# Two more query chunks in fp32 through TensorE during the first batch's weight wait, and the second batch's keys on a dense, later grid

## The chip, the cores and the metric

The kernel runs on one core of one Trainium2 chip. The metric is the device time of one execution in microseconds (us), lower is better. Times are given for several executions of the same kernel; the profile describes one execution.

## The reference, cut to what matters

The reference is an agent attention followed by a mixture of experts in which every token goes to one expert. There are 4 batches of 11456 tokens with 128 channels, 49 agents in each batch, and 8 experts with an inner width of 1024.

```python
def _attn_ref(q, k, v, agents):
    scale = 1.0 / np.sqrt(q.shape[-1])
    def sm(a, b):
        s = scale * (a @ b.transpose(0, 2, 1))
        e = np.exp(s - s.max(-1, keepdims=True))
        return e / (e.sum(-1, keepdims=True) + 1e-09)
    agent_v = sm(agents, k) @ v
    return sm(q, agents) @ agent_v
...
logits = x @ w_gate                      # x: attention output, all tokens
expert_idx = np.argmax(logits, axis=1)
gate_w = softmax(logits).max over experts, with 1e-09 in the divisor
for e in range(E):
    out[mask_e] = gate_w * (relu(x[mask_e] @ w1[e]) @ w2[e])
```

## The kernel before, in words

**Tiles.** A batch is cut into 12 chunks: 11 of 1024 tokens (128 partitions by 8 tokens) and one of 192 tokens. Batch by batch the kernel loads keys, values and queries chunk by chunk. From keys and values it forms the 49 agent values; from those it guesses the expert that most tokens of the batch will take (`choose`), loads that expert's two weight matrices (`weights_load`, tiles `w1e` and `w2e`) and prepares them (`weights`, six parts). Each query chunk gives a matrix `M` of exponentials (`qscores`, `qexp`, `esplit`, `eturn`), which is the moving operand of the expert's first layer.

**Steps.** The main work of a batch is 184 steps: 23 groups of 512 tokens by 8 slices of the inner width. In a step `layer1` writes one PSUM tile with two matmuls (lines 1300 and 1301), ScalarE makes the high half of the ReLU (line 1306), VectorE the low half (line 1307), and five steps later `layer2` does twelve small matmuls (line 1321). Tokens that the guessed expert doesn't serve are handled after the last batch.

**How a chunk is prepared.** In mode `A` (all keys and queries but some of the first batch) ScalarE squares and sums the chunk (`squares`, line 359), two small VectorE operations make a power-of-two scale (lines 230 and 234), ScalarE and VectorE write a high and a low fp16 half (`split`, lines 393 and 395), a DMA transpose on the SP queue turns both halves (`turn_over`, line 421, tile `hT`), and TensorE forms the scores from 24 fp16 matmuls (`scores`, lines 462 to 464). In mode `X` (first batch: some key chunks, and the first `NQ` query chunks) none of that is done: TensorE transposes the fp32 chunk against an identity (`transposed`, line 441), ScalarE copies one half out of PSUM (line 447) and VectorE the other (line 445), and TensorE forms the scores in fp32 (line 460).

**Order.** Every piece of work is put into a queue of events with a time in steps (`at`); negative times are before the first step. The events are traced in the order of those times. After that the compiler's planner orders each engine's instructions from this priority and from costs of its own, so a ready instruction may stand ahead of an older one that still waits for data. A batch's steps take the times 0 to 183 for the first batch, 184 onwards for the second. `uses` lists all chunk loads in the order of their times; a load call also issues the next ones (eight in all while the first batch is prepared, three later). The loads and the two weight matrices share one pool of eleven buffers (tag `ld`). In the first batch `gate["D"]` holds the splits of the first two batches back until `choose` has found the expert, and `gate["S"]` holds their DMA transposes back until the load of `w2e` is issued. Small PSUM tiles, and the scores of mode `X` queries, come from a pool of two buffers (`psS`).

**The first batch.** Its keys start at time -200, its values at -168, `choose` stands at -142, the six weight parts at -139 to -131.5. Query chunk 0 is prepared at -172 in mode `X`. Query chunks 1 and 2 are prepared in mode `A` at times -15 and -7, chunks 3 to 11 at 2, 15, 28 and so on. The keys of the second batch are prepared at -27, -18, -9, 0, 9 and so on up to 72, with their scores 12 steps later.

Of the kernel before, what the change touches and what calls it, by code (L numbers as in the profile page):

```python
# [29 lines left out]


MODES = {'k': 'XCCXCCXCCXCX', 'v': 'F', 'q': 'X'}
NQ = 1


HI = [{'k': 'A', 'v': 'A', 'q': 'A'}, {'k': 'A', 'v': 'A', 'q': 'A'}]
# [6 lines left out]
PKM = False  # L43


KS0, KT0, KL0, VT0, VL0, QS0, QT0, QL0 = -200, 2, 4, 2, 1, -172, 3, 2.5
VE, T1, TF0, TF1, TL, TLM, Q0 = 12, 1.75, 3, 1.5, 18, 10, 2

KS, KT, VT, VL, VL4, TW0, TW1, DW = -211, 9, 5.3, 8, 5, 8, 2.5, 1
QA, QB, QC, QB3, KL, LL, UD, RG, D1, DL = -23, 8, 13, 10.5, 12, 9.5, 2, 0.7, 0.5, 0  # L50

KS1 = []

KLL, LLL = 12, 11
LX, LMG, LSP = 8, 4, 2.5
# [21 lines left out]
def agent_moe_kernel(ctx, tc, q, k, v, agents, wg, w1, w2, out):  # L77
    nc = tc.nc
# [141 lines left out]
    def queued(x):  # L220
        return tc.issue_after(gate[x].ins) if x in gate else nullcontext()
# [46 lines left out]
    def pick(x, c):  # L268
        return x[c % len(x)]
# [6 lines left out]
    def at(t, f, *a):  # L276
        count[0] += 1
        heapq.heappush(events, (t, count[0], f, a))
# [4 lines left out]
    def turns(gen, t, dt, n):  # L283
        for i in range(n):
            at(t + i * dt, next, gen, None)
# [3 lines left out]
    def attention(b):  # L289
        st = state[b]  # L290
        base = b * steps
        first, last = b == 0, b + 1 == B

        how = {}
        for x in "kvq":
            for c in range(NCK):
                how[x, c] = pick(MODES[x], c) if first and (x != "q" or c < NQ) else "A"

# [168 lines left out]
        S = [None] * NCK  # L467
# [234 lines left out]
        def esplit(c):  # L702
            _, p, t = chunks[c]
            e, m2 = Es[c], mm[c % len(mm)]
            if pick(M1E, c) == "D":
                nc.vector.tensor_copy(m2[:p, :t, :A], e[:p, :t, :])
            else:
                nc.scalar.copy(m2[:p, :t, :A], e[:p, :t, :])
            eng = nc.gpsimd if pick(M2L if last else M2E, c) == "P" else nc.vector
            eng.tensor_tensor(m2[:p, :t, 64:64 + A], e[:p, :t, :], m2[:p, :t, :A], op=ALU.subtract)  # L710
            after(0 if first and c == 0 else DTE, eturn, c, m2)

        def eturn(c, m2):
            _, p, t = chunks[c]
            m = mpool.tile([P, 8, P], F16, tag="M", name="M")
            nc.sync.dma_start_transpose(m[:, :t, :p], m2[:p, :t, :].rearrange("p t a -> p (t a)"))
            Ms[c] = m

        def logits(c):
# [137 lines left out]
        def use(t, src, c):  # L857
            uses.append((base + t, b, src, c))

        def prepare(t, src, c):  # L860
            at(base + t, squares, src, c)
            at(base + t + (0 if first else D1), total, src, c)
            at(base + t + (0.5 if first else UD), total2, src, c)
            at(base + t + (1 if first else D1 + 0.3 if src != "v" else UD + 1), transposed if how[src, c] in "CX" else split, src, c)

        ks, kt, kl, vt, vl = (KS0, KT0, KL0, VT0, VL0) if first else (KS, KT, KL, VT, VL)
        dl = 0 if first else DL
        ka = KS1[0] - base if b == 1 and KS1 else ks
        at(base + ka - 3, agent_squares)
        at(base + ka - 2, agent_split)  # L870
        for c in range(NCK):
            t = KS1[c] - base if b == 1 and c < len(KS1) else ks + kt * c
            use(t, "k", c)
# [7 lines left out]
        for c in range(NCK):  # L881
            t = tv + vt * c
# [20 lines left out]
        tw += w0 + 5 * w1_  # L903
        for c in range(NCK):
            if first and c < NQ:
                t, ql_ = QS0 + QT0 * c, QL0
            else:
                t = (Q0 + QC * (c - 3) if first and c > 2 else QA + QB * c if c < 3 else
                     QA + 2 * QB + (QB3 if last else QC) * (c - 2))
                ql_ = KLL if last and c > 2 else KL  # L910
            use(t, "q", c)
            prepare(t, "q", c)
            at(base + t + ql_, qscores, c)
            at(base + t + ql_ + (0 if first and c < NQ else DL), qexp, c)
            at(base + t + ql_ + 3, esplit, c)
            tl = max(t + ql_ + (TL if first and c < NQ else LLL if last and c > 2 else LL), ta + (TLM if first else 4) + c / 2)
            end = min([x for x in starts if x > c] + [NCK]) - 1
            c0 = max(x for x in starts if x <= c)
            late_ = c0 * 16 + LAG + 8 - 6 * RG - 1 - LMG - LSP * (end - c)
            late_ = min(late_, (LT3 if last else LT) - 6 * RG - 1.5 - LSP * (NCK - 1 - c))  # L920
            tl = max(tl, min(tl + LX, late_))
            at(base + tl, logits, c)
            if c + 1 in starts or c == NCK - 1:
                turns(route(c), base + tl + 1, RG, 6)
                tf = max(tl + 1 + 6 * RG, tw + 1)
                at(base + tf, factors, c)
                c0 = max(x for x in starts if x <= c)
                assert tf < c0 * 16 + LAG + 8, (b, c, tf)
# [446 lines left out]
    for b in range(B):  # L1375
        attention(b)
        steps_of.append(experts(b))
        turns(steps_of[b], b * steps, 1, steps + LAG + 2)
        turns(leftover_ranks(b), b * steps + (LT3 if b + 1 == B else LT), LTS3 if b + 1 == B else LTS, 6)

    for j in range(2 * E):
        b, i = divmod(j, -(-2 * E // (B - 1)))
# [14 lines left out]
    while events:  # L1397
# [3 lines left out]
        with ExitStack() as held:  # L1401
            if now[0] > 0 and queue:
                held.enter_context(tc.issue_after(queue[-1]))
            if not (f is next and a[0] in steps_of):
                for x, s in ((1, SLP), (2, SLA), (3, SLD)):
                    p = next((p for p in reversed(paced) if p[0] <= now[0] - s), None)
# [76 lines left out]
```

## Time and profile before

| | us |
|---|---|
| median of 3 runs | 1130.12 |
| lowest and highest | 1129.23, 1131.7 |
| the profiled execution | 1129.85 |
| its span, first to last instruction | 1128.1 |

| engine | busy us | share of the span |
|---|---|---|
| TensorE matmul (PE) | 1021.4 | 91% |
| VectorE (DVE) | 1000.8 | 89% |
| ScalarE (ACT) | 829.3 | 74% |
| GpSimd (POOL) | 214.5 | 19% |

Shares over the whole span are averages over stages with different limits. The page also has the span in 40 slices of 28.2 us, each digit a tenth of busy time; PEclk is the granted TensorE clock in tenths of full speed. Times within the span are counted from its first instruction. Clock 1.00 stands for 2.4 GHz and 0.50 for 1.2 GHz. Matmuls are pipelined, so the lengths of single matmuls overlap and don't add up. A wait names what released the engine.

### The profile page before, as it was taken

How to read it: one execution, taken by the hardware profiler on the slowest of the kernel's cores; microseconds unless marked ns; L12 is line 12 of the kernel's file. 1: busy time of each engine (PE TensorE's matmuls, PEld its weight loads, DVE VectorE, ACT ScalarE, POOL GpSimd, SP SyncE). 2: the span in 40 equal slices, each digit the busy share in tenths (PEclk: the TensorE clock that was granted, in tenths of full speed). 3: DMA queues.
4: the chain of work that ended last, by engine and by line, in shares of the span. 5: the costliest groups of instructions: out<-in, count | busy, mean ns of one | idle time of the engine just before them, and what ended most of it. 6: DMA issues, size and time to landing. Idle time of an engine off the chain costs nothing. (4 is left out here: it accounts for less than half of the span.)

```text
span 1128.1 us, 35718 instructions
## 1 busy us (share of the span) xinstructions
PE 1021.4 (91%) x14575; PEld 823.6 (73%) x14575; DVE 1000.8 (89%) x2372; ACT 829.3 (74%) x1495; POOL 214.5 (19%) x369
## 2 busy tenths in 40 slices
PE   7847999989899999999889999999999988989995
PEld 7725877777776778777667778777777766767795
DVE  5876998999888998998788998998899998799894
ACT  6556887888787887888677887888677665656681
POOL 1300000134400011233300011234200113110133
PEclk9866999999999999999899999999999999999998
DMA  8579789633399998645299998634467653433470
GB/s 324 182 231 211 196 179 206 168 107 119 108 268 205 212 209 204 158 127 182 84 241 223 198 214 204 170 114 159 119 177 167 148 112 84 133 102 125 119 249 14
DMA packets 263592, 190.49 MB, mean 169 GB/s; under 512 B 215433, under 2 KB 228226, under 8 KB 263424
## 3 DMA queue, kind: packets, MB, share of 16 engines
q1 hardware_dynamic: 261856, 185.92, 64.0%
q0 software_dynamic: 1568, 2.25, 1.0%
q8 instruction: 115, 1.88, 0.7%
q14 instruction: 53, 0.43, 0.1%
HBM read 99.75 MB, written 36.43 MB: 121 GB/s over the span
## 5 line engine op out<-in xcount | busy, mean ns | idle before, releaser
L1321 PEld LDWEIGHTS <-hh 128*128 128x128 f16 x8640 | 550.4, 99 | 168.7 <-issue 8.9
L1321 PE MATMUL py<-w2h,hh 128*128 128x128 f16 (+1 forms) x5760 | 609.8, 220 | 1.1 <-issue 0.9
L1321 PE MATMUL py<-w2l,hh 128*128 128x128 f16 (+1 forms) x2880 | 526.5, 220 | 1.2 <-issue 1.2
L1306 ACT ACTIVATE hh<-ph 128x512 f16<-128x512 f32 (+1 forms) x728 | 407.8, 581 | 146.6 <-PE ph L1301 139.1
L1307 DVE SCALAR_TENSOR_TENSOR hh<-ph,hh 128x512 f16<-128x512 f32 (+1 forms) x736 | 478.2, 665 | 29.4 <-ACT hh L1306 26.6
L1300 PE MATMUL ph<-M,Ah 128*128 128x512 f16 (+1 forms) x736 | 276.7, 376 | 35.3 <-DVE hh L1307 23.6
L1301 PE MATMUL ph<-M,Al 128*128 128x512 f16 (+1 forms) x736 | 276.7, 376 | 0.2 <-DVE Al L814 0.2
L395 DVE SCALAR_TENSOR_TENSOR hl<-ld,mul,hl 128x1024 f16<-128x1024 f32 (+1 forms) x119 | 148.5, 1255 | 14.6 <-ACT hl L393 12.0
L393 ACT ACTIVATE hl<-ld,mul 128x1024 f16<-128x1024 f32 (+1 forms) x119 | 128.7, 1091 | 29.9 <-DVE mul L234 26.8
L359 ACT ACTIVATE jk<-ld 128x1024 f16<-128x1024 f32 (+1 forms) x126 | 126.2, 1001 | 5.2 <-DMA ld<-in_k_dram 3.9
L237 POOL TENSOR_SCALAR div<-hb,bits 128x1 int32<-128x1 int32 (+1 forms) x90 | 27.0, 300 | 470.3 <-DVE hb L230 443.9
L1301 PEld LDWEIGHTS <-Al 128*128 128x128 f16 x736 | 71.8, 98 | 36.0 <-issue 33.8
L1300 PEld LDWEIGHTS <-Ah 128*128 128x128 f16 x736 | 73.5, 100 | 9.3 <-DMA M<-mm 4.9
L462 PEld LDWEIGHTS <-hT 128*128 128x128 f16 (+1 forms) x622 | 52.7, 99 | 23.5 <-DMA hT<-hl 22.8
L462 PE MATMUL ps_s<-agh,hT 128*128 128x49 f16 x558 | 52.6, 186 | 13.8 <-DMA hT<-hl 12.0
L1334 DVE TENSOR_TENSOR yo<-py,cs 128x512 f32<-128x512 f32 (+1 forms) x92 | 61.5, 669 | 2.9 <-PE py L1321 2.8
L463 PEld LDWEIGHTS <-hT 128*128 128x128 f16 (+1 forms) x622 | 51.6, 99 | 3.2 <-issue 2.9
L464 PE MATMUL ps_s<-agh,hT 128*128 128x49 f16 x558 | 52.3, 186 | 0.0
L463 PE MATMUL ps_s<-agl,hT 128*128 128x49 f16 x558 | 52.3, 186 | 0.0
L464 PEld LDWEIGHTS <-hT 128*128 128x128 f16 (+1 forms) x622 | 51.3, 98 | 0.0
L556 POOL TENSOR_TENSOR es<-es,S 128x392 f32<-128x392 f32 (+1 forms) x33 | 33.4, 1011 | 92.8 <-ACT S L537 76.1
L699 ACT ACTIVATE E<-E,ln,div 128x392 f32<-128x392 f32 (+1 forms) x47 | 32.4, 689 | 14.1 <-DVE E L693 13.2
(319 smaller groups left out, 1344.6 us busy)
## 6 DMA issues: line engine op xcount, KB each, us to landing
ld<-in_k_dram SPq DMA_DIRECT2D x44, 512.0 KB
ld<-in_v_dram SPq DMA_DIRECT2D x44, 512.0 KB
ld<-in_q_dram SPq DMA_DIRECT2D x44, 512.0 KB
out_dram<-yo SPq DMA_DIRECT2D x88, 256.0 KB
w1e<-in_moe_w_dram SPq DMA_DIRECT2D x18, 512.0 KB
w2e<-in_moe_w_dram SPq DMA_DIRECT2D x18, 512.0 KB
exps<-E SPq DMA_DIRECT2D x44, 196.0 KB
wn<-in_moe_w_dram SPq DMA_DIRECT2D x16, 512.0 KB
```

Source lines behind the costliest of these rows:

```text
L359: nc.scalar.activation(jk[:p, :t * D], x[:p, :t, :].rearrange("p t d -> p (t d)"), AF.Square, accum_out=ss[:p])
L393: nc.scalar.activation(hi[:p, :t, :], x[:p, :t, :], AF.Copy, scale=m)
L395: nc.vector.scalar_tensor_tensor(lo[:p, :t, :], x[:p, :t, :], m, hi[:p, :t, :], op0=ALU.mult, op1=ALU.subtract)
L462: nc.tensor.matmul(o, x[:, 0, i, :p], AG["h"], start=True, stop=False)
L463: nc.tensor.matmul(o, x[:, 0, i, :p], AG["l"], start=False, stop=False)
L464: nc.tensor.matmul(o, x[:, 1, i, :p], AG["h"], start=False, stop=True)
L1300: x1 = nc.tensor.matmul(ph[:, :nn], st['Ah'][:, f, :], m, start=True, stop=False)
L1301: nc.tensor.matmul(ph[:, :nn], st['Al'][:, f, :], m, start=False, stop=True)
L1306: x2 = nc.scalar.activation(hh[:, 0, :nn], ph[:, :nn], AF.Relu)
L1307: x3 = nc.vector.scalar_tensor_tensor(hh[:, 1, :nn], ph[:, :nn], 0.0, hh[:, 0, :nn], op0=ALU.max, op1=ALU.subtract)
L1321: mm_ = lambda l, r, **k: nc.tensor.matmul(o, l, r, skip_group_check=True, **k)
L1334: nc.vector.tensor_tensor(yo[:p, :n, :], py[:p, :n * D].rearrange("p (i d) -> p i d", d=D), cs.unsqueeze(2).broadcast_to([p, n, D]), op=AL ...
```

## The change

`NQ` becomes 3, so that query chunks 1 and 2 of the first batch take mode `X`, at times -146 and -145, with scores 2.5 later and `esplit` 5.5 later. That is after the last values (-145) and around the first parts of `agentvalues` (-144.25 to -140.5) and `choose` (-142). The DMA transpose of their `M` is held behind the load of `w2e`, and their `logits` stand at 6 and 8 before a later rule moves them to 14 and 16 (before: 14.5 and 19.8). Query chunks 3 to 11 move 6 steps later, to 8, 21 and so on. The keys of the second batch are prepared at -10, -3, 5, 13 and so on, every 8 steps up to 77, and their agents three steps ahead of that, at -13.

```diff
-NQ = 1
+NQ = 3
...
-KS0, KT0, KL0, VT0, VL0, QS0, QT0, QL0 = -200, 2, 4, 2, 1, -172, 3, 2.5
-VE, T1, TF0, TF1, TL, TLM, Q0 = 12, 1.75, 3, 1.5, 18, 10, 2
+KS0, KT0, KL0, VT0, VL0, QS0, QL0 = -200, 2, 4, 2, 1, (-172, -146, -145), 2.5
+VE, T1, TF0, TF1, TL, TLM, Q0 = 12, 1.75, 3, 1.5, 18, 10, 8
...
-KS1 = []
+KS1 = [-10, -3] + [5 + 8 * i for i in range(10)]
...
         def eturn(c, m2):
...
-            nc.sync.dma_start_transpose(m[:, :t, :p], m2[:p, :t, :].rearrange("p t a -> p (t a)"))
+            with queued("S") if first and 0 < c < NQ else nullcontext():
+                nc.sync.dma_start_transpose(m[:, :t, :p], m2[:p, :t, :].rearrange("p t a -> p (t a)"))
...
             if first and c < NQ:
-                t, ql_ = QS0 + QT0 * c, QL0
+                t, ql_ = QS0[c], QL0
...
             tl = max(t + ql_ + (TL if first and c < NQ else LLL if last and c > 2 else LL), ta + (TLM if first else 4) + c / 2)
+            if first and 0 < c < NQ:
+                tl = 4 + 2 * c
```

## Rows read from the trace of the kernel before

**Rows 1.** The page's slices of 28.2 us each, by engine.
```profile
PE   7847999989899999999889999999999988989995
...
PEclk9866999999999999999899999999999999999998
```

**Rows 2.** Busy time of each engine, clock and DMA share in stretches.
```profile
core 0: us, PE busy (x) PEld busy (x) DVE busy (x) ACT busy (x) POOL busy (x), PEclk, DMA share, GB/s
58.00:62.00 4.00, 2.22 (x12) 1.48 (x12) 2.98 (x16) 0.00 (x0) 0.00 (x0) 0.84 0.97 397
62.00:66.00 4.00, 0.55 (x2) 0.50 (x2) 1.36 (x9) 0.00 (x0) 0.00 (x0) 0.50 0.52 167
...
72.00:120.00 48.00, 32.40 (x430) 24.55 (x429) 37.00 (x85) 35.99 (x58) 4.85 (x13) 0.75 0.98 194
120.00:187.00 67.00, 65.67 (x1008) 52.27 (x1006) 64.45 (x136) 54.20 (x95) 5.17 (x12) 1.00 0.87 200
```

**Rows 3.** First-layer matmuls (line 1300, one a step) in two stretches.
```profile
72.00:120.00 48.00, 8.78 (x22) 2.08 (x20) 0.75 0.98 194
120.00:187.00 67.00, 20.04 (x53) 5.16 (x53) 1.00 0.87 200
```

**Rows 4.** Waits of PE from 72 to 120 us: total, times, longest.
```profile
PE ps_s L462 <- DMA hT<-hl: 5.8, 3, 2.3
PE ph L1300 <- DVE mul L234: 4.5, 1, 4.5
PE ps_y L462 <- DMA hT<-hl: 3.3, 2, 2.7
```

**Rows 5.** Groups of VectorE from 72 to 120 us: busy, mean ns.
```profile
L395 DVE SCALAR_TENSOR_TENSOR hl<-ld,mul,hl 128x1024 f16<-128x1024 f32 x10 | 12.6, 1281 | 1.4 <-ACT hl L393 1.3
...
L691 DVE TENSOR_REDUCE mq<-ps_y 128x8 f32<-128x392 f32 x3 | 1.7, 563 | 1.0 <-PE ps_y L464 1.0
L693 DVE TENSOR_TENSOR E<-ps_y,mq 128x392 f32<-128x392 f32 x3 | 1.7, 559 | 0.0
L234 DVE TENSOR_SCALAR mul<-hb 128x1 int32<-128x1 int32 x11 | 1.6, 147 | 0.1
L230 DVE TENSOR_SCALAR hb<-ss 128x1 int32<-128x1 int32 x10 | 1.5, 145 | 1.0 <-ACT jk L359 1.0
...
L706 DVE CAST mm<-E 128x392 f16<-128x392 f32 x3 | 1.1, 363 | 0.6 <-ACT E L699 0.6
...
L710 DVE TENSOR_TENSOR mm<-E,mm 128x392 f16<-128x392 f32 x1 | 0.6, 561 | 0.0
```

**Rows 6.** VectorE low halves of splits (line 395), same two stretches.
```profile
120.00:187.00 67.00, 12.80 (x10) 1.00 0.87 200
```

**Rows 7.** Order of time on PE: fp32 transposes and scores of whole chunks.
```profile
13.84 1.95 PE L441 MATMUL pxT<-ident,ld 128*128 128x128 f32 x8
...
19.87 1.88 PE L460 MATMUL ps_s<-agT,xF 128*128 128x49 f32 x16
21.62 1.07 PE L441 MATMUL pxT<-ident,ld 128*128 128x128 f32 x8
...
41.96 3.65 PE L460 MATMUL ps_s<-agT,xF 128*128 128x49 f32 x16
45.53 12.42 PE L577 MATMUL pv<-ld,S 128*49 128x128 f32 x180
```

**Rows 8.** VectorE's half of the copy of a transposed fp32 chunk.
```profile
L445 DVE COPY xF<-pxT x5: 683/685/691, 7.5 to 37.4; 128x512 f32<-128x512 f32 x5
```

**Rows 9.** Order of time on PE from the last values to the first step.
```profile
60.13 0.39 PE L780 MATMUL ps_small<-wg_sb,avs 128*128 128x8 f32 x2 [1.00 <-DVE avs L634]
...
66.57 2.08 PE L807 MATMUL pa<-w1e,av 128*128 128x512 f32 x2 [3.44 <-DMA w1e<-in_moe_w_dram]
```

**Rows 10.** Busy times and DMA share just ahead of the weights.
```profile
56.00:62.00 6.00, 4.22 (x48) 3.29 (x44) 4.81 (x20) 0.00 (x0) 0.00 (x0) 0.89 0.98 401
62.00:63.00 1.00, 0.43 (x2) 0.46 (x2) 0.39 (x3) 0.00 (x0) 0.00 (x0) 0.50 0.04 16
```

## The prediction

> **What bounds the kernel now.** I read the slices of the page first [rows 1]. From the fifth slice on PE is at 8 to 9 tenths at a clock of 10, and the first four stand out: 7, 8, 4, 7 with the clock at 9, 8, 6, 6. In the third and fourth slice, 56 to 113 us, the engines wait for the guessed expert's weights and then fill the pipeline of steps. The stretches show what lies there [rows 2]. From 62 to 66 us PE is busy for 0.55 of 4.00 us, VectorE for 1.36 and ScalarE not at all. From 72 to 120 us PE is busy for 32.40 of 48, VectorE for 37.00, at a clock of 0.75. From 120 to 187 us PE has 65.67 of 67 and VectorE 64.45, at full clock: two engines close to their limit. The steps show the same [rows 3]: 22 first-layer matmuls in the 48 us, or 2.18 us a step, against 53 in 67 us, or 1.26 us.
>
> The ramp is slow because 10 chunks are split in it [rows 5], nearly one for every two steps. The next 53 steps have 10 more [rows 6]. The low half alone costs VectorE 1.28 us a chunk, and TensorE then waits for the transposes of these chunks: 5.8 and 3.3 us for `hT`, and 4.5 us for a VectorE operation behind other work [rows 4]. So two stretches can give time, the 4 us before the weights and the 48 us after them. What is worth something in the second is VectorE time, since VectorE has less idle time there (11.0 us) than PE (15.6 us) [rows 2].
>
> **Step 1: the ramp sheds work.** Two of the ten split chunks are queries 1 and 2, which leave the fp16 path; two or three more are second-batch keys, which move from -27, -18, -9 and 0 to -10, -3, 5 and 13. By step 75 the same keys and queries have been started in both versions: the twelfth key at 72 before and 77 after, the ninth query at 67 before and 73 after. So I balance VectorE over 72 to 187 us, the first 22 + 53 = 75 steps [rows 3]. Its busy time there is 37.00 + 64.45 = 101.45 us of 115 [rows 2]. What leaves for each query chunk is the low half 1.281, the two scale operations 0.145 and 0.147, the row maximum 0.563, the subtraction 0.559 and the cast 0.363 [rows 5], 3.06 us; one of the two also has its low part of `M` on VectorE, 0.561. Together 6.7 us, so 94.8 us remain. If the ramp were as dense as the stretch behind it, 64.45 of 67 or 96%, this would take 98.5 us instead of 115: a gain of 16.5 us, the upper bound of this term.
>
> It won't be that dense at once. The keys at -10 and -3 are still split before the first step, the third comes at 5, and each needs its DMA transpose. PE's five waits for `hT` in the ramp are 9.1 us, 1.8 each [rows 4]; I leave three of them, 5.5 us, of which VectorE works off some backlog in about a quarter, and charge 4. That makes 12.5 us. The lower bound is that no idle time is recovered and only the hidden work goes: 0. In the likeliest case I take 9 to 16.5, with 9 if all of the 7.5 us between the 16.5 and the 9.1 us of waits stays.
>
> The DMA transposes of the two query chunks go too, and the share of DMA in the ramp is 0.98 [rows 2]; I count nothing for that, since it is the same wait for `hT`.
>
> **Step 2: what is put in front of the weights.** Each query chunk brings eight fp32 transposes and sixteen score matmuls to PE. The same on other chunks took 1.07 and 1.88 us at full clock, 1.95 and 3.65 at half [rows 7], so the two chunks are 5.9 us at full clock and 11.2 at half. On VectorE come the copy of one half, 0.685 [rows 8], and the maximum, the subtraction and the cast, 1.49 [rows 5], so 2.2 us a chunk, plus 0.56 for one low part: 4.9 us. The idle time from 58 to 66 us is 1.78 + 3.45 = 5.2 us on PE and 1.02 + 2.64 = 3.7 us on VectorE [rows 2]. On paper nearly all fits in. But the scores of both chunks are written ahead of `choose` (-143.5 and -142.5 against -142), share its two small PSUM buffers, and whatever runs ahead of `choose` pushes the load of the weights back. PE has only the 1.0 us of its wait there free [rows 9]. Bounds: 0.5 us, if the planner puts them into the wait for `w1e` of 3.44 us [rows 9] and only a few operations get in the way, and 5.9 - 1.0 = 4.9 us if all of it precedes `choose` at full clock; at half clock 11.2 - 1.0 = 10.2. The values ahead of it keep PE busy for 12.42 us without a break [rows 7], so the full clock is the nearer case. As the planner starts what is ready, I take the middle of 0.5 and 4.9, 2.5 us of delay.
>
> **The clock, as a rule.** The two products of `w1e` with the agent values take 2.08 us each pair at a clock of 0.50, after a wait of 3.44 us [rows 2, 9]. The Trainium skill, page "TensorE: Matmul & The Clock Gate", section "Loop structure matters more than you think", says that a wait for DMA between matmuls sends the array to the half clock and that other dense work keeps it fast. No row has this wait filled with other matmuls. By that rule the pairs would take half, some 1 us each as an estimate, and the delay of 2.5 us would be about 1.5; I keep 2.5.
>
> **A rule against the change.** The Trainium skill, page "FP8 and Floating Point Precision", section "TensorE Precision Notes", puts true fp32 at four passes through the array. By that, as an estimate, eight transposes of 128 columns and eight scores of 49 at 2.4 GHz are 1.71 + 0.65 = 2.4 us a chunk, against 2.95 from the rows; the delay would be a little smaller. I go by the rows.
>
> **Step 3: loads.** In written order queries 1 and 2 come first now, and as they call for loads further ahead, two more chunks are asked for before the weights. The DMA engines are 0.98 busy from 56 to 62 us at 401 GB/s and 0.04 in the microsecond behind [rows 10]. A chunk of 512 KB at 401 GB/s is 1.3 us, the two 2.6 us. The free microsecond and the delay of step 2 cover it: 0, with 1.6 us as the upper bound if `choose` isn't delayed at all.
>
> **Step 4: what is late next.** The last key of the second batch comes 5 steps later, with scores at 89 instead of 84, and the key maximum at 86 to 88, behind which the second batch's values wait, is where it was. Its nearest predecessor, key 10, has its scores at 81, five steps or 6.3 us [rows 3] ahead. Queries 3 to 11 are 6 steps later, and a group of steps starts every 16, with their `M` due later than that. Cost 0; if the maximum has to wait, the price is one key's VectorE work, 1.28 + 0.29 [rows 5], about 1.6 us. The logits of queries 1 and 2 stand at 14 and 16 and only get earlier. The later move of ten keys adds no work, it makes steps 22 to 77 denser, which the balance of step 1 holds already.
>
> **Sum.** 12.5 - 2.5 = 10.0 us. The profiled execution took 1129.85 us, so 1119.9; the median of the runs is 0.27 us above it, so 1120.1. The likeliest case's own range is a gain of 9 - 4.9 = 4 to 16.5 - 0.5 = 16 us, 1114 to 1126.
>
> **Rivals.** *The ramp stays slow.* The transposes of the keys stay, on a DMA that is 0.98 busy, and PE waits for them in order. For: 9.1 us of waits for `hT` [rows 4]. Against: two of ten chunks lose the transpose altogether. Gain of step 1 then about 4 instead of 12.5, time 1126 to 1130, about 1128.5.
>
> *The chain in front of the weights takes it back.* Queries 1 and 2 ahead of `choose` at the half clock, as query 0's scores had it (3.65 us [rows 7]): 10.2 us of delay, gain 2, 1128.
>
> *Slower.* The same place, but nothing hides: 11.2 us of PE plus VectorE's 4.9 and the 2.6 us of loads, one behind the other because both small PSUM buffers are held until VectorE has read them, 18.7 us against a gain of 12.5: 1136. It decides when the delay of the load of `w1e` passes 12.5 us. Against it: VectorE's operations overlap PE's, and the loads overlap both.
>
> *It doesn't do what it says.* The planner may place queries 1 and 2 after the weights have landed. Then the 4.9 us of VectorE work return to the ramp and there is no delay: 12.5 - 4.9 = 7.6 us, 1122.5, inside the likeliest range.
>
> *More.* The ramp becomes as dense as the rest, the clock stays up: 17 us or more, 1112.
>
> **Chances.** Likeliest case, with the planner's rival in it, 0.65; the slow ramp 0.12; the chain at half clock 0.10; slower 0.08; more 0.05. A change of 0.2%, 2.3 us, is about what a measurement of this kernel can tell from none. Half of the two middle rivals, 0.11, falls within it; faster then is 0.65 + 0.05 + 0.11 = 0.81, slower 0.08. The range runs from 1112 to 1129, which leaves out the slower rival and the far ends of the others.
>
> **What would show it.** Right: matmuls of lines 441 and 460 between 50 and 67 us; ScalarE or VectorE no longer splitting query chunks in the ramp (line 395: six or seven by step 22, not ten); 75 steps done by about 177 us; `w1e` landing 0.5 to 5 us later than at 66.5. Wrong: the first step after 80 us; waits for `hT` in the ramp of 9 us or more; VectorE's idle time in the first 75 steps still above 10 us; or a new wait at the second batch's key maximum.

## The result and the profile after

The changed kernel takes 1136.53 us (median of 20 runs) against 1129.25 us before (20 runs on the same chip): ratio 1.0059, 95% interval 1.0047 to 1.0072, or 6.7 us slower. One of its 20 runs took 2587.18 us and is left out of the ratio. The forecast was 10 us faster. The profiled execution took 1137.81 us (span 1136.1 us). In the changed kernel the lines behind `eturn` stand one lower and those of the steps three lower: the first-layer matmul is line 1303 (1300 before), the logits are line 726 (725), `choose` is line 781 (780), the products with `w1e` are line 808 (807).

The slices of the page, beside [rows 1]:

```profile
PE   7877989989898999999888999999999998989995
PEclk9869989999899999999899999999999999999998
```

The third slice, from 57 us, went from 4 to 7, and the clock of the fourth from 6 to 9: the ramp did become denser. But slice 6, 142 to 170 us, now has an 8 for PE and an 8 for the clock, and slice 11, 284 to 312 us, an 8 for the clock, where the kernel before had 9s. Something was lost behind the ramp. The stretches, beside [rows 2]:

```profile
core 0: us, PE busy (x) PEld busy (x) DVE busy (x) ACT busy (x) POOL busy (x), PEclk, DMA share, GB/s
58.00:62.00 4.00, 4.00 (x45) 3.82 (x39) 3.40 (x8) 1.17 (x2) 0.00 (x0) 1.00 1.03 419
62.00:66.00 4.00, 3.31 (x23) 3.21 (x22) 1.46 (x5) 0.62 (x1) 0.00 (x0) 0.76 0.95 387
72.00:120.00 48.00, 38.86 (x472) 27.83 (x472) 38.03 (x99) 35.19 (x62) 3.31 (x10) 0.87 0.69 163
120.00:187.00 67.00, 60.74 (x919) 48.69 (x917) 58.88 (x118) 50.11 (x87) 3.70 (x11) 0.95 0.92 199
```

And the first-layer matmuls, one a step, beside [rows 3]:

```profile
72.00:120.00 48.00, 10.65 (x27) 2.70 (x27) 0.87 0.69 163
120.00:187.00 67.00, 18.04 (x47) 4.63 (x47) 0.95 0.92 199
```

From 72 to 120 us the changed kernel makes 27 steps, five more than before, although its first step comes later. From 120 to 187 us it makes 47, six fewer; PE, which was busy for 65.67 of these 67 us, is now busy for 60.74. The waits of PE say what ended its idle time; first from 72 to 120 us (beside [rows 4]):

```profile
PE ps_s L462 <- DMA hT<-hl: 5.0, 3, 2.9
PE pa L808 <- DMA w1e<-in_moe_w_dram: 2.0, 1, 2.0
```

then from 120 to 187 us, all of them:

```profile
PE ps_y L726 <- DMA M<-mm: 4.9, 1, 4.9
PE ps_s L462 <- DMA hT<-hl: 1.2, 1, 1.2
```

The 9.1 us of waits for `hT` in the ramp have become 5.0. In the dense stretch there is one new wait, 4.9 us, of the logits for a transposed `M`.

To see where the time goes over the whole kernel, I took the start of the n-th first-layer matmul as the time of step n. The table gives it for the kernel before, and for each other version the difference to it (us, from one profiled execution each; the versions are described below):

| version | step 0 | 8 | 24 | 56 | 64 | 80 | 104 | 144 | 160 | 207 | 735 |
|---|---|---|---|---|---|---|---|---|---|---|---|
| before | 71.9 | 99.1 | 123.0 | 163.4 | 173.4 | 194.9 | 225.6 | 279.9 | 303.8 | 370.5 | 1069.9 |
| after | +7.5 | -9.8 | -6.8 | -6.6 | +0.7 | +2.9 | +5.1 | +5.2 | +9.0 | +9.5 | +6.8 |
| e1 queries only | +4.7 | -8.3 | -6.4 | -5.8 | +1.2 | -0.5 | +0.7 | +2.4 | +3.5 | +6.5 | +2.7 |
| e2 keys only | +0.4 | -6.5 | -10.3 | -7.6 | -7.3 | -8.0 | -6.8 | -6.9 | -6.6 | -4.6 | -6.6 |
| e3 late queries undone | +6.3 | -6.6 | -8.9 | -6.6 | -6.3 | -6.7 | -5.5 | -5.5 | -5.5 | -4.4 | -7.4 |
| e6 late queries alone | -0.4 | -1.5 | -3.4 | -3.2 | +3.0 | +1.4 | +2.7 | +2.8 | +6.9 | +7.8 | +11.8 |
| e7 query 5 back | +6.0 | -10.9 | -9.6 | -7.7 | -7.2 | -4.6 | -2.5 | -2.4 | +1.7 | +2.3 | +3.3 |
| e9 5 and 9 to 11 back | +7.2 | -9.6 | -8.6 | -5.1 | -4.6 | -3.6 | -1.6 | -2.4 | -2.4 | -0.1 | -1.9 |
| e13 ranks held | +5.6 | -11.6 | -8.7 | -8.3 | -1.3 | +1.0 | +3.2 | +3.3 | +1.1 | +0.8 | +4.1 |
| e14 both mended | +5.5 | -11.7 | -8.6 | -7.2 | -5.7 | -5.3 | -3.1 | -3.0 | -5.2 | -6.2 | -6.9 |

The row of the changed kernel reads: 7.5 us behind at the first step, 9.8 ahead at step 8, 6.6 ahead at step 56. Then it loses 7.3 us between steps 56 and 64, 4.4 between 64 and 104, and 3.8 between 144 and 160 (the kernel before is itself slow just ahead of step 152, where the changed one wins 1.9 back, so that 5.7 are lost from 152 to 160). The gain of the ramp is there, and is given back at two or three places far behind it.

**The place at step 56.** The order of time on PE, with the wait in brackets behind the operation that waited:

```profile
156.82 0.38 PE L1303 MATMUL ph<-M,Ah 128*128 128x512 f16 x1
162.14 0.38 PE L726 MATMUL ps_y<-Gs,M 128*128 128x18 f16 x8 [4.94 <-DMA M<-mm]
162.37 0.59 PE L1304 MATMUL ph<-M,Al 128*128 128x512 f16 x1
```

and SP's DMA queue just ahead of it, in order of time:

```profile
152.20 1.91 SPq L421 DMA_TRANSPOSE hT<-hl  x1
154.16 1.02 SPq L1412 DMA_DIRECT2D exps<-E  x1
155.27 3.66 SPq L421 DMA_TRANSPOSE hT<-hl  x1
159.02 1.26 SPq L717 DMA_TRANSPOSE M<-mm  x1
```

The logits of query 5, the last of the group that starts at step 48, stand in front of the next steps on PE, and wait for the turn of `M` (its DMA transpose). The source of that turn was complete early. These are the last two operations that write it, on VectorE and GpSimd:

```profile
149.75 0.35 DVE L706 CAST mm<-E 128x392 f16<-128x392 f32 x1
...
150.19 0.91 POOL L710 TENSOR_TENSOR mm<-E,mm 128x392 f16<-128x392 f32 x1 [1.24 <-DVE mm L706]
```

So `mm` was there at 151.10, and its turn began at 159.02, 7.9 us later: in SP's queue two transposes of split chunks and a store stand ahead of it, and the second transpose is held until VectorE has made its source:

```profile
156.12 1.28 DVE L395 SCALAR_TENSOR_TENSOR hl<-ld,mul,hl 128x1024 f16<-128x1024 f32 x1
```

`hl` is complete at 157.40, the transpose lands at 158.93, the turn of `M` at 160.28, and PE runs at 162.14. After the wait the granted clock is 0.50 from 162 to 166 us: the first-layer matmul behind it (line 1304) takes 0.59 us instead of 0.38. In the kernel before, the `mm` of query 5 was complete at 150.50 us, and its turn came 1.9 us later, more than 3 us ahead of the logits (157.9):

```profile
152.35 2.04 SPq L716 DMA_TRANSPOSE M<-mm  x1
```

**The place at step 152.** GpSimd, in order of time; lines 939 to 956 are the first batch's leftover ranks, line 556 the second batch's sums of its exponentials, line 237 a scale:

```profile
289.79 1.78 POOL L939 TENSOR_TENSOR C<-oh,npri 128x720 f32<-128x720 f32 x1 [5.53 <-DVE rs L766]
...
297.95 2.74 POOL L952 TENSOR_TENSOR cp<-cp,C 128x8 f32<-128x8 f32 x10
300.65 0.39 POOL L556 TENSOR_TENSOR es<-es,S 96x98 f32<-96x98 f32 x1
301.00 0.48 POOL L952 TENSOR_TENSOR cp<-cp,C 128x8 f32<-128x8 f32 x2
301.44 1.48 POOL L954 TENSOR_TENSOR C<-C,cp 128x704 f32<-128x704 f32 x1
```

and the waits of all engines from 296 to 312 us that belong to it:

```profile
ACT jk L323 <- DVE sa L322: 3.3, 1, 3.3
...
PE ps_small L325 <- ACT jk L323: 2.6, 1, 2.6
...
DVE e L610 <- POOL es L556: 1.3, 1, 1.3
```

The last sum, an operation of 0.39 us, stands behind ranks that began at 289.79, after GpSimd had waited 5.53 us for the routing of the last group. VectorE waits for the sum, ScalarE for VectorE (`jk` squares the third batch's agents), PE for ScalarE. The kernel before has ranks ahead of a sum of the second batch too, only earlier and with less behind them (PE waits 1.9 us there):

```profile
278.83 1.77 POOL L936 TENSOR_TENSOR C<-oh,npri 128x720 f32<-128x720 f32 x1 [3.08 <-DVE rs L765]
...
291.21 1.01 POOL L556 TENSOR_TENSOR es<-es,S 128x392 f32<-128x392 f32 x1
```

**The place between steps 64 and 104.** Most of the 4.4 us, 3.5, are lost from step 76 to step 80. PE waits there 0.89 us for a low half and 1.06 us for VectorE's sum of the logits:

```profile
193.86 0.26 PE L1324 MATMUL py<-w2h,hh 128*128 128x128 f16 x1 [1.06 <-DVE Ld L728]
```

Behind the waits the granted clock is 0.50 from 194 to 196 us.

### The profile page after: what moved, and what is told of

Read it like the earlier page. It is cut to its first block, busy times and chain, and to the rows that moved or that the text cites. A ratio compares the mean times of both kernels' runs of the same rounds, so it can differ in the third digit from the quotient of the medians.

```text
span 1136.1 us, 35697 instructions
## 1 busy us (share of the span) xinstructions
PE 1029.6 (91%) x14575; PEld 830.1 (73%) x14575; DVE 999.5 (88%) x2368; ACT 825.8 (73%) x1491; POOL 214.3 (19%) x367
## 3 DMA queue, kind: packets, MB, share of 16 engines
q8 instruction: 115, 1.88, 0.7%
## 5 line engine op out<-in xcount | busy, mean ns | idle before, releaser
L395 DVE SCALAR_TENSOR_TENSOR hl<-ld,mul,hl 128x1024 f16<-128x1024 f32 (+1 forms) x117 | 145.4, 1248 | 15.9 <-ACT hl L393 13.7
L1304 PEld LDWEIGHTS <-Al 128*128 128x128 f16 x736 | 71.9, 98 | 37.2 <-issue 35.4
L1303 PEld LDWEIGHTS <-Ah 128*128 128x128 f16 x736 | 73.7, 100 | 10.9 <-DMA M<-mm 5.8
L462 PEld LDWEIGHTS <-hT 128*128 128x128 f16 x606 | 49.9, 97 | 15.2 <-DMA hT<-hl 14.3
L463 PEld LDWEIGHTS <-hT 128*128 128x128 f16 x606 | 48.8, 97 | 1.4 <-issue 1.1
L464 PEld LDWEIGHTS <-hT 128*128 128x128 f16 x606 | 48.5, 97 | 0.0
```

The source lines that it names most:

```text
L395: nc.vector.scalar_tensor_tensor(lo[:p, :t, :], x[:p, :t, :], m, hi[:p, :t, :], op0=ALU.mult, op1=ALU.subtract)
L462: nc.tensor.matmul(o, x[:, 0, i, :p], AG["h"], start=True, stop=False)
L463: nc.tensor.matmul(o, x[:, 0, i, :p], AG["l"], start=False, stop=False)
L464: nc.tensor.matmul(o, x[:, 1, i, :p], AG["h"], start=False, stop=True)
L1303: x1 = nc.tensor.matmul(ph[:, :nn], st['Ah'][:, f, :], m, start=True, stop=False)
L1304: nc.tensor.matmul(ph[:, :nn], st['Al'][:, f, :], m, start=False, stop=True)
```

## The experiments

The two theories at the outset: the cost lies in front of the weights (queries 1 and 2 put ahead of `choose`), or it lies in the other queries, which come six steps later because `Q0` went from 2 to 8. Ratios are to the kernel before, run on the same chip, with a 95% interval.

**e1 and e2: the two halves of the change.** The changed kernel with the keys' old times, and the kernel before with the keys' new times:

```diff
 # e1, in the changed kernel
-KS1 = [-10, -3] + [5 + 8 * i for i in range(10)]
+KS1 = []
 # e2, in the kernel before
-KS1 = []
+KS1 = [-10, -3] + [5 + 8 * i for i in range(10)]
```

> The change without its key part: the second batch's keys stay at -27, -18, -9 and so on, queries 1 and 2 go in fp32, queries 3 to 11 six steps later. Theory (the fp32 work of the two queries ahead of the choice of expert puts the weights 5 to 6 us later, and the sixth query chunk's M comes too late for its logits, about 5 us): both stay, and the ramp gets less relief than in the whole change, so the first step at 77 to 80 us and a time of 1134 to 1142. Rival (the denser, later keys are what costs): they are gone, so 1120 to 1128.

> The key part alone: the second batch's keys at -10, -3, 5, 13 and so on, one fp32 query chunk, queries 1 to 11 where they were. Theory: no delay ahead of the weights (first step at 72 to 73 us) and no late M at the sixth query, while the ramp is relieved of two or three key chunks, so 1122 to 1128. Rival (later and denser keys cost): 1132 to 1138, with the loss between steps 60 and 110.

Measured: e1 1134.77 us, 1.0044 (1.0020 to 1.0067); e2 1123.37 us, 0.9928 (0.9901 to 0.9956). The keys alone are a gain of 8 us, and the first step stays where it was (+0.4). The queries' part alone is a loss of 5 us. It has the 7 us loss between steps 56 and 64 (from -5.8 to +1.2) too, so that loss doesn't need the new keys.

**e3, e4, e5: which half of the queries' part.** e3 puts queries 3 to 11 back at their old times, e4 moves the two fp32 queries behind `choose` in written order, e5 does both:

```diff
 # e3 and e5
-VE, T1, TF0, TF1, TL, TLM, Q0 = 12, 1.75, 3, 1.5, 18, 10, 8
+VE, T1, TF0, TF1, TL, TLM, Q0 = 12, 1.75, 3, 1.5, 18, 10, 2
 # e4 and e5
-KS0, KT0, KL0, VT0, VL0, QS0, QL0 = -200, 2, 4, 2, 1, (-172, -146, -145), 2.5
+KS0, KT0, KL0, VT0, VL0, QS0, QL0 = -200, 2, 4, 2, 1, (-172, -141, -140), 2.5
```

> The whole change, but queries 3 to 11 stay where they were before it (2, 15, 28 and so on). Theory: the delay ahead of the weights stays (first step at about 79 us), the wait of PE for the M of the sixth query chunk, 4.9 us and 7 us of lost lead between steps 56 and 64, is gone: 1128 to 1131. Rival (that wait is only where a lack of VectorE time shows): the loss moves elsewhere, 1135 to 1138.

> The whole change, but queries 1 and 2 are prepared at -141 and -140, behind the choice of expert, not at -146 and -145. Theory: the weights land 5 us earlier, the first step comes at 73 to 75 us instead of 79.3, and the time falls by 4 to 6 us to 1130 to 1133. Rival (the work only moves from ahead of the weights to behind them, so the steps that follow start as late): first step at 78 us or more, 1135 to 1138.

> The whole change with queries 1 and 2 behind the choice of expert (-141, -140) and queries 3 to 11 where they were before the change. Theory (the late queries cost most, the delay ahead of the weights the rest): the first step at about 74 us, no 5 us wait for M, the lead of about 9 us at step 56 kept: 1119 to 1123. Rival (what is won at the first step is lost in the ramp, as it was between the first step and step 4 with the queries late): no better than 1123 to 1125.

Measured: e3 1123.66 us, 0.9934 (0.9908 to 0.9961); e4 1136.16 us, 1.0034 (1.0018 to 1.0051); e5 1125.29 us, 0.9938 (0.9915 to 0.9961). In e4 `choose` runs at 60.97 and the first step at 74.1 us, 5.2 us sooner than in the changed kernel; at step 56 2.3 us of that are left, and the wait for `M` is still there (5.0 us). In e3 the first step is as late as 78.2 us, and the kernel is 14 us faster than the changed one (1.0059 - 0.9934 = 0.0125 of 1129.25, some 3 us either way by the two intervals). In e3's SP queue the turn of query 5's `M` comes well ahead, and no wait for `M` is left:

```profile
144.53 1.29 SPq L717 DMA_TRANSPOSE M<-mm  x1
```

The theory of the place in front of the weights falls; what costs the time is `Q0`. e5 bears that out from the other side: its first step comes at 74.3 us, 3.9 us sooner than e3's, its next 75 steps take 4.5 us longer, and the two times can't be told apart.

**e6: `Q0` alone.** The kernel before with only that number changed:

```diff
-VE, T1, TF0, TF1, TL, TLM, Q0 = 12, 1.75, 3, 1.5, 18, 10, 2
+VE, T1, TF0, TF1, TL, TLM, Q0 = 12, 1.75, 3, 1.5, 18, 10, 8
```

> The kernel before with nothing but queries 3 to 11 six steps later. Theory (the late queries alone cost 11 to 13 us): 1139 to 1144, with a wait of PE for M near step 56. Rival (they cost only where the ramp has been made faster): 1129 to 1133.

Measured: 1140.35 us, 1.0071 (1.0048 to 1.0093). With nothing else changed the six steps cost 8 us, and both places show the same waits; these are from e6, from 120 to 200 us and from 284 to 312 us:

```profile
PE ps_s L725 <- DMA M<-mm: 4.6, 1, 4.6
```

```profile
POOL C L936 <- DVE rs L765: 5.5, 1, 5.5
...
ACT jk L323 <- DVE sa L322: 3.3, 1, 3.3
```

**e7, e8, e9: which of the nine queries.** In the changed kernel, query 5 alone goes back (e7), queries 3 to 5 (e8), or 5 and 9 to 11 (e9):

```diff
-                t = (Q0 + QC * (c - 3) if first and c > 2 else QA + QB * c if c < 3 else
+                t = (Q0 - 6 * (c == 5) + QC * (c - 3) if first and c > 2 else QA + QB * c if c < 3 else
 # e8: - 6 * (c < 6); e9: - 6 * (c == 5 or c > 8)
```

> The whole change, but of queries 3 to 11 only query 5 keeps its old place; the others stay six steps late. Theory (its M is the one that its logits wait for): the loss of 7 us between steps 56 and 64 is gone, the later losses stay: 1128 to 1132. Rival (all losses follow from that one stall): 1122 to 1125. Rival (another query takes its place): 1135 to 1138.

> The whole change, but queries 3, 4 and 5 keep their old places and only 6 to 11 come six steps later. Theory (besides the stall at query 5 the late last queries cost 5 to 6 us, mostly between steps 104 and 160): 1127 to 1131. Rival (only the stall at query 5 counts): 1122 to 1125.

> The whole change, but queries 5, 9, 10 and 11 keep their old places; 3, 4, 6, 7 and 8 stay six steps late. Theory (two deadlines are missed: the M of query 5 near step 56, and the routing of the last group, queries 9 to 11, which makes GpSimd's leftover ranks late near step 152): both losses gone, 1124 to 1129, at most 2 us lost between steps 152 and 160. Rival (the late loss comes from the mean lateness of the queries, not from the last group): 1131 to 1134, as with query 5 alone put back.

Measured: e7 1132.37 us, 1.0006 (0.9990 to 1.0022); e8 1130.86 us, 0.9978 (0.9953 to 1.0002); e9 1126.89 us, 0.9966 (0.9946 to 0.9985). Query 5 alone is worth 0.0053, 6.0 us, and the loss between steps 56 and 64 is gone (-7.7, -7.2). The last group is worth 0.0040, 4.5 us, on top, and the loss from 144 to 160 is gone (-2.4, -2.4). e8 fell within its theory, but its time can't be told apart from e7's.

**e10 and e12: the ranks behind the sum.** If the last group costs time because its routing delays the ranks, and these stand in front of the sum on GpSimd, then holding the ranks behind that sum should help, with the queries as late as they are. In e10, `gate["es", b]` keeps the last sum of a batch (line 556), and the first batch's ranks start 8 steps later, 5 apart:

```diff
+        with (tc.issue_after(gate["es", 1].ins) if b == 0 else nullcontext()):
...
-        turns(leftover_ranks(b), b * steps + (LT3 if b + 1 == B else LT), LTS3 if b + 1 == B else LTS, 6)
+        turns(leftover_ranks(b), b * steps + (LT3 if b + 1 == B else LT + 8 * (b == 0)), LTS3 if b + 1 == B else LTS - (b == 0), 6)
```

> The whole change; only the first batch's leftover ranks on GpSimd are held behind the second batch's last sum of exponentials. Theory (those ranks, come late, stand on GpSimd ahead of that sum, for which VectorE, ScalarE and then PE wait near step 152): 4 to 6 us of loss between steps 152 and 160 go, the wait at query 5 stays: 1130 to 1133. Rival (the stretch near step 152 is slow for another reason): 1135 to 1138.

Measured: 1136.42 us, 1.0059 (1.0033 to 1.0086), not the gain that was expected. The sum no longer waits, but the loss between steps 152 and 168 is still 4.1 us (counted from step 144, 1.1 us against the changed kernel's 3.8, since the held ranks win 3.0 us just ahead of step 152), for the next operation on GpSimd now stands behind the ranks, the scale of the third batch's agents (line 237):

```profile
301.40 1.47 POOL L955 TENSOR_TENSOR C<-C,cp 128x704 f32<-128x704 f32 x1
...
303.14 0.21 POOL L237 TENSOR_SCALAR div<-hb 128x1 int32<-128x1 int32 x1
```

VectorE's next operation needs it:

```profile
303.38 0.15 DVE L331 TENSOR_SCALAR bits<-div 128x1 f32<-128x1 int32 x1 [3.32 <-POOL div L237]
```

e12 is e10 with query 5 back in place as well (the edit of e7).

> The whole change with query 5 alone at its old place and the leftover ranks held behind the last sum of exponentials. Theory: both losses go, though the other queries stay six steps late: 1125 to 1129. Rival (late queries cost in other places too): 1131 to 1136.

Measured: 1128.87 us, 0.9987 (0.9972 to 1.0002), with the same wait for the scale (3.31 us): within the theory by its number, while the wait behind the ranks had only moved.

**e11: the fp32 queries alone.** The changed kernel with the old keys and the old `Q0` (the edits of e1 and e3).

> Only queries 1 and 2 in fp32; queries 3 to 11 and the second batch's keys where they were before the change. Theory (two query chunks less in the ramp give 6 to 8 us there, the first step comes 5 to 6 us later but that costs 2 us at most): 1124 to 1128. Rival (the later first step counts in full): 1128 to 1133.

Measured: 1127.72 us, 0.9986 (0.9967 to 1.0005): no difference that can be told from none, 1.6 us at best guess. With the same fp32 queries and old keys, the late queries (e1, 1.0044) cost 6.5 us.

**e13 and e14: the ranks behind the scale too.** As e10, but held behind the third batch's agent scale, which comes after the sum, and starting 14 steps later, 4 apart; e14 has query 5 back in place as well:

```diff
-        nc.gpsimd.tensor_scalar(div[:p, :n].bitcast(I32), hb[:p, :n],
+        gate["div"] = nc.gpsimd.tensor_scalar(div[:p, :n].bitcast(I32), hb[:p, :n],
...
             AG["mul"], div = scale_bits(sab, P, 1, "as")
+            gate["as", b] = gate["div"]
...
+        with (tc.issue_after(gate["as", 2].ins) if b == 0 else nullcontext()):
```

> The changed kernel with the first batch's leftover ranks held on GpSimd behind the third batch's agent scale, the operation that stood behind them when they were held behind the second batch's last sum alone. If the loss of 5.7 us at steps 152 to 160 is only what stands behind the ranks on GpSimd, it goes now: about 1131 to 1133 us, ratio 1.002, no wait of the agent scale or of the sum behind ranks. If it comes from the group of queries 9 to 11 being late in another way (its steps' matrix work itself, or whatever GpSimd operation comes next), the time stays at 1135 to 1137, ratio 1.005.

> The same, with query 5 back at its old time as well, so that both waits are taken out while the other eight queries stay six steps late. If the two waits are the whole of the two losses: like the run with queries 5 and 9 to 11 back in place, ratio 0.9966, about 1126 us. If holding the ranks only moves the block again: like the run with the ranks held behind the sum and query 5 back, ratio 0.9987, about 1128.5 us.

Measured: e13 1133.53 us, 1.0010 (0.9991 to 1.0029), where the kernel before took 1132.46 on that chip; e14 1126.12 us, 0.9942 (0.9918 to 0.9966). GpSimd in e13 (its lines stand one or two lower):

```profile
292.18 0.39 POOL L557 TENSOR_TENSOR es<-es,S 96x98 f32<-96x98 f32 x1 [1.58 <-ACT S L538]
292.54 0.37 POOL L565 TENSOR_TENSOR eh<-S,eh 96x98 f16<-96x98 f32 x1
300.03 0.21 POOL L237 TENSOR_SCALAR div<-hb 128x1 int32<-128x1 int32 x1 [7.12 <-DVE hb L230]
300.32 1.78 POOL L941 TENSOR_TENSOR C<-oh,npri 128x720 f32<-128x720 f32 x1
```

The sum and the scale wait for their own sources only, the ranks come behind them, and the loss between steps 144 and 160 has turned into a gain (+3.3, +1.1), though the last queries are as late as in the changed kernel. So the GpSimd queue is the cause at this place. e14 holds the ranks and still has eight of the nine queries late, and it is 13.2 us (0.0117) faster than the changed kernel, against the 14.1 us that undoing `Q0` brings. Not all of that is repair: e13 and e14 gain 2.2 us on the kernel before from step 144 to 160, where e3 gains nothing, as holding the ranks also takes out the wait that the kernel before has there. By that reckoning about 11 of the 14.1 us are the two waits, and the loss between steps 64 and 104 stays in e14 (2.6 us).

The fastest versions are e2 and e3, at 0.9928 and 0.9934; the intervals don't separate them from each other or from e14 and e5. All four are faster than both kernels, clear of the intervals.

## Why the prediction was wrong

**The step that failed is Step 4, "what is late next".** It said that queries 3 to 11 are six steps later, that a group starts every 16, that the `M` of a group is due later than that, and it put the cost at 0. The runs put it at 8 us alone (e6, 1.0071), 6.5 us with the fp32 queries (e1 against e11) and 14.1 us within the change (e3 against the changed kernel). The due times that the step looked at are those of the group; what it didn't look at is that the last query of a group has far less room than the first. By the written times (`QC` = 13, `KL` = 12, `LL` = 9.5), query 5 is prepared at 34 instead of 28, so its logits move only from 51.8 to 55.5: the rule that spaces them out already had no more than 3.7 steps to give, and the other 2.3 come out of the room between the turn of `M` and the logits. For the last group the logits move from 135.5 to 138.3, and the ranks, which are written for step 144, find their routing done later: GpSimd waits 5.53 us for it, where it waited 3.08 in the kernel before.

**Why a small shift cost so much** is in the two queues. The turn of `M` waited on nothing but its place: 7.9 us in SP's queue behind transposes of other chunks, one of them waiting for VectorE (`M` has six buffers, `MP` = 6, and this is the sixth `M`). The sum of 0.39 us waited behind ranks that hold GpSimd from 289.79 to past 303 us. The gains are shown: e7 removes the first (6.0 us) and e13 the second (5.5 us, some 2 of them a wait that the kernel before has as well), e14 both (13.2 us; the intervals of the three are wide enough for the 1.7 us between that and their sum). That the queue did it is shown by a run for GpSimd (e13); for SP's queue it is read from the trace, and no run moved the transposes ahead of `M`.

**Step 1 was right**, in mechanism and nearly in size, where the late queries don't cover it. In e3 the 75 steps from the first take 103.9 us, in the kernel before 115.8: 11.9 us less, against a sum of 12.5. VectorE is busy for 5.7 us less in them (the forecast had 6.7) and idle for 7.4 us instead of 13.5. In the changed kernel itself low halves of splits are down from ten to seven from 72 to 120 us, with five more steps in it, and the waits for `hT` fall from 9.1 to 5.0 us, where the forecast left 5.5. What the prediction didn't see is who brings the net gain. The keys do (e2, all of 0.9928), and the fp32 queries next to nothing (e11, 0.9986): with them the 75 steps are 6.9 us shorter, but the first step comes 4.3 us later. The two parts don't add; e3, which has both, is no faster than e2.

**Step 2 was sized too small**: 2.5 us of delay, where `choose` comes 6.28 us later (66.41 against 60.13 in [rows 9]). Of these, 1.24 were there before the changed place: the values begin at 46.77 instead of 45.53 [rows 7]. The other 5.0 are about the upper bound of the step, 4.9: the planner put all four pieces ahead of `choose`. PE from 58 us to the first step:

```profile
58.50 1.09 PE L441 MATMUL pxT<-ident,ld 128*128 128x128 f32 x8
...
59.81 1.05 PE L441 MATMUL pxT<-ident,ld 128*128 128x128 f32 x8
60.70 1.88 PE L460 MATMUL ps_s<-agT,xF 128*128 128x49 f32 x16
...
63.50 3.11 PE L460 MATMUL ps_s<-agT,xF 128*128 128x49 f32 x16 [0.69 <-DVE av L628]
66.41 0.56 PE L781 MATMUL ps_small<-wg_sb,avs 128*128 128x8 f32 x2
...
73.36 3.78 PE L808 MATMUL pa<-w1e,av 128*128 128x512 f32 x4 [2.02 <-DMA w1e<-in_moe_w_dram]
...
79.34 0.82 PE L1303 MATMUL ph<-M,Ah 128*128 128x512 f16 x3 [1.35 <-ACT Ah L814]
```

The durations of the rows held: 1.09, 1.05 and 1.88 us at full clock, 3.11 for the second scores, partly at half. But the size hardly matters, as e4 and e5 show: in e4, of 5.2 us less delay 1.5 are left at step 4 and 2.3 at step 56, and e5 is no faster than e3. So the delay and the gain of Step 1 are not two terms to be added, as the sum has them: a first step that comes sooner finds a longer ramp. In e4 PE waits for VectorE behind the first steps (0.73 and 1.46 us between 79 and 82 us); whether that is all of it wasn't tried.

**The clock.** The wait is filled now: PE is busy for 3.31 us from 62 to 66 us instead of 0.55, and the granted clock there is 0.76 instead of 0.50. From 66 to 72 us, where PE is busy for 2.76 us, it is 0.50 again. The four products with `w1e` take 3.78 us, where a pair took 2.08 before [rows 9], and 2.02 us of the wait are left ahead of them. The Trainium skill, page "TensorE: Matmul & The Clock Gate", section "Loop structure matters more than you think", lets dense work in place of a wait keep the array fast. The trace agrees for 58 to 62 us (clock 1.00, 0.84 before) and shows no gain at the products. In e4, which has fp32 scores ahead of the first pair of products and transposes between the pairs, the first pair still takes 2.08 us, and the second runs at a clock of 0.98 (70 to 72 us):

```profile
71.27 1.10 PE L808 MATMUL pa<-w1e,av 128*128 128x512 f32 x2
```

So the 1 us a pair that the prediction estimated was seen for that one.

**The rivals.** "Slower" gave 1136 us, which is the number measured, but by another mechanism: it put the price in front of the weights, and e3 has that in full and is 7.5 us faster than the kernel before. None of the rivals held what happened. The forecast of what would show a wrong prediction names a first step after 80 us, waits for `hT` of 9 us, VectorE idle for over 10 us in the first 75 steps, and a wait at the key maximum. The first two and the last didn't come; VectorE's idle time did (115 - 38.03 - 58.88 = 18.1 us from 72 to 187 us, 13.6 before), and 3.4 us of the 4.5 more are VectorE's wait for the logits that waited for `M`. Of the signs of being right, the fp32 matmuls came where they were expected (58.50 to 66.6 us); step 75 starts at 188.3 us instead of 177, and the products with `w1e` 6.8 us later than before, more than the 0.5 to 5 forecast.

**The account.** Forecast a gain of 10.0. Without the late queries (e3) the change gains 7.5 us, the late queries cost 14.1, and the sum is 6.7 us slower. Of e3's 7.5, step 75 has 5.5 already: 11.9 of Step 1 less 6.3 of delay. Why it ends 2.5 below the forecast isn't shown; the delay alone doesn't explain it, for e5 has 3.9 us less of it and gains no more.

**What stays open.** From step 64 to 104 the changed kernel loses 4.4 us and e14 2.6, while e2 and e3 lose 0.5 and 0.8. e1 and e6, late queries with the old keys, don't have it (0.5 and 0.3 us gained). So it comes with late queries and the new keys together. The trace puts it mostly at steps 76 to 80, where e14 has the same waits of PE (0.62 and 1.06 us) at a clock of 1.00 and loses 1.6 us, the changed kernel 3.5; no run took these waits out. Between steps 598 and 621 some profiles differ by 2 to 4 us that no part of the change reaches; the table is of one execution each, and the ratios, over all runs, don't rest on them.

## What to carry to other kernels

When a stage of a hand-written order is moved, go through each operation that it issues to the last one of its group, and read the room of that one: on the queue (which transfers, waiting for whom, are ahead of it?) and at the next user, not against the due time of the group. In a queue that is worked off in order, a short operation on the path can cost as much as what stands ahead of it: here 0.39 us on GpSimd and 1.26 us on SP's queue were worth 5.5 and 6.0 us. Don't add a gain behind a delay to the delay itself before you know that the one leaves the other alone. And split a change before judging it: one of its three parts brought the whole gain, one nothing that could be measured, one the loss.

## What the runs showed of the hardware that was not expected

- A DMA transpose whose source was complete at 151.10 us started at 159.02, behind one in SP's queue whose source VectorE completed at 157.40.
- Holding back a chain of small operations on GpSimd moved the block to the next operation behind it (e10: from a sum to a scale, VectorE waited 3.32 us); only when both stood ahead of the chain was the time back (e13).
- With the wait for the weights filled by fp32 matmuls the granted clock was 1.00 up to 62 us, 0.76 from 62 to 66 and 0.50 from 66 to 72, and the second chunk's scores took 3.11 us instead of 1.88.
- 5.2 us less delay of the first step (e4) were worth 1.5 us by step 4 and 2.3 us by step 56.
